# Loading a broadcast bias at another place of the POOL queue, in a linear-attention and gMLP block on Trainium2

## The chip, the cores and the metric

The kernel runs on one core of one Trainium2 chip. The core has a matrix engine (TensorE, PE in the profile), a vector engine (VectorE, DVE), an activation engine (ScalarE, ACT), a general engine (GpSimd, POOL) and SyncE (SP), which here only issues transfers. All five run their own instruction streams and wait for one another through semaphores. Transfers issued by SP, ACT or POOL share 16 DMA engines. The metric is the device time of one execution in microseconds (us), the median of several runs. The measurement of this kernel can tell a change of about 0.2%, some 0.5 us, from none.

## The reference

Two pre-normalised blocks, one after the other, on 2048 rows of 512 features (bf16). The first is linear attention with 32 heads of 16, the second a gated MLP whose gate mixes over the rows.

```python
x  = A_x
h  = x + A(layernorm(x))            # A: q,k,v = x @ wqkv; phi(t) = where(t>0, t+1, exp(t)) + 1e-6
                                    #    o = phi(q) @ (phi(k).T @ v) / (phi(q) . sum(phi(k)) + 1e-6); o @ wo
h2 = h + B(layernorm(h))
def B(x):
    z  = gelu(x @ w_in)             # 512 -> 1792
    z1 = z[..., :896]
    z2 = layernorm(z[..., 896:])
    g  = einsum('ts,sf->tf', w_sp, z2) + b_sp[:, None]   # mixes the 2048 rows; b_sp: one value per row
    return (z1 * g) @ w_out
```

The change concerns the load of `b_sp`, the mixing bias.

## The kernel before

The 2048 rows are 16 row tiles of 128, in four groups of four. The stages, which overlap:

- **x**: statistics of x on DVE, normalisation, transposition into `xT`.
- **k, q**: projections on PE, phi by ACT (Exp and Relu, L727 and L729) and DVE (L730, L733, L736). ACT and DVE pass the intermediate values through three buffers `e` (the pool `EB`).
- **kv and denominators**: L790 to L911.
- **h**: PE multiplies phi(q) by a matrix prepared from k, v and wo (L933, 8 matmuls for two row tiles). DVE adds x (L938) and makes the statistics (L577, L581). POOL makes 1/sqrt(var + eps) for two tiles at a time: an addition (L596), a power of -1/2 (L598, the "reciprocal root"), and with L631 and L632 the negative mean. ACT normalises into one of four buffers `xn` (L623), and SP transposes that by DMA into `hT` (L642).
- **z2**: PE projects each row tile of h (L968: 4 matmuls of 512 columns and 4 of 384), ACT applies gelu (L973), DVE makes statistics (L977, L581), POOL the roots (L596, L598 again), and DVE normalises in place (L612).
- **z1**: computed transposed, in 28 blocks of 4 matmuls (L999), gelu on ACT (L1004).
- **mixing**: PE multiplies z2 by the transposed `w_sp` (L1038, 28 sums over 16 row tiles each); DVE adds the bias (L1045, which reads `bsp`) and multiplies by z1. The first sum goes two row tiles at a time, in order, as z2 comes in. `w_sp` is transposed by 64 DMA transposes on SP (L1014, 16 for each group of output rows; the first mixing waits for all 16 of its group).
- **output**: L1056 projects with `wout`, L1062 adds h, SP stores.

The bias is broadcast to all 128 partitions, 512 KB in all. Its buffer lies in the store of the `e` buffers, as do the buffers `gb` and `o_` of the mixing and the output:

```python
bs_v = View(s_eb, 0, [S], BF16)
BS = Pool(1, lambda s, w: bs_v.ap, over=[EB])
```

`over=[EB]` means that the first operation on a tile of `BS` waits for every operation on every `e` tile. The load is a DMA issued on POOL, so POOL waits for this before it goes on with its queue.

The order of the work is written out. Each call of `op` adds an operation to a list, numbered as the program makes it; `ORDER` is a list of these numbers, and `schedule` gives each engine its operations in that order. `SLOT` holds, for each tile in the order of its first use, the buffer that it gets: a PSUM bank, an `e` or an `xn` buffer, and so on. `_waits` derives the semaphores from the data. The arguments `bias`, `cost` and `after` do not reorder anything here: `after` only demands that `ORDER` keep one operation behind another.

POOL also issues the loads of the weights (`wv`, `wo`, `win`, `wout`). The load of `wout` waits for the last transpose into `hT`, since `load` gets it as `behind`.

Of the kernel before, what the change touches and what calls it, by code (L numbers as in the profile page):

```python
# [10 lines left out]
P = 128  # L11
# [38 lines left out]
]  # L50
SLOT = [
# [6 lines left out]
]  # L58


# [294 lines left out]
def bass_sequential_preLN__linear_attn_block__mixer_gmlp__prompt_kernel(  # L355
# [11 lines left out]
    _, S, D = A_x.shape  # L367
# [61 lines left out]
    def small(shape, dtype):  # L429
        n = (int(np.prod(shape)) * mybir.dt.size(dtype) + GRAIN - 1) // GRAIN * GRAIN  # L430
        o = at[0]
        at[0] += n
        return View(s_sm, o, shape, dtype)
# [33 lines left out]
    BS = Pool(1, lambda s, w: bs_v.ap, over=[EB])  # L467
# [8 lines left out]
    def bank(i):  # L476
        return lambda a: a[:, i, :]
# [4 lines left out]
    g = Program(nc)  # L482
# [8 lines left out]
    def dve_c(n, mode=1):  # L491
        return 0.08 + 0.00103 * n / mode


    def load(eng, name, dst, src, nbytes, bias=0.0, behind=(), cost=0.5):
        o = op(eng, cost, lambda e: e.dma_start(dst.ap(), src), w=[dst], dma=(name, False), nbytes=nbytes,
               bias=bias, land=2.3)
        for p in behind:
            o.deps[p] = True
        return o  # L500
# [94 lines left out]
    def rstd_pool(var, dst, n):  # L595
        op("pool", 0.18, lambda e: e.tensor_scalar(dst.ap(), var.ap(), EPS_LN, None, op0=ALU.add), r=[var], w=[dst])  # L596
        h = nhalf[0:n]
        return op("pool", 0.665, lambda e: e.tensor_tensor(dst.ap(), dst.ap(), h.ap(), ALU.pow), r=[dst, h], w=[dst])  # L598
# [316 lines left out]
    for gs in DEN:  # L915
# [4 lines left out]
                    q_proj(gq, f)  # L920
        den(gs)

    for gq in range(NG):
        g.bias = -GROUP * gq
        for p in (2 * gq, 2 * gq + 1):
            t = Tile(PS, 2)
            for ti in range(2):
                n = 2 * p + ti
                l = pqT[gq][:, (n % TPG) * P:(n % TPG + 1) * P]

                def mm(e, t=t, ti=ti, l=l):
                    for c in range(KD):
                        i = e.matmul(t(bank(ti)).ap(), lhsT=l.ap()[:, c, :], rhs=mw[c, :].ap(), start=(c == 0),  # L933
                                     stop=(c == KD - 1))
                    return i
                op("pe", 4 * MM, mm, r=[l, mw.all()], w=[t()])
            d = x[2 * p:2 * p + 2, :]
            op("dve", dve_c(1024), lambda e, t=t, d=d: e.tensor_tensor(d.ap(), t().ap(), d.ap(), ALU.add),  # L938
               r=[t(), d], w=[d])
            rs = small([2], FP32)  # L940
            for n in (2 * p, 2 * p + 1):
                stats(x[n, :], Row(st_h, n))
                aggr(Row(st_h, n), 6)
            rstd_pool(st_h[2 * p:2 * p + 2, 7], rs.all(), 2)
            nm = small([2], FP32)
            if 2 * p in N2_ACT:
                minus(st_h[2 * p:2 * p + 2, 6], rs.all(), nm.all())
            for i in range(2):
                n = 2 * p + i
                t = Tile(XN)  # L950
                if n in N2_ACT:
                    normalise_act(t(), x[n, :], rs[i:i + 1], nm[i:i + 1])
                else:
                    normalise(t(), x[n, :], Row(st_h, n), 6, rs[i:i + 1])
                transposed(n, t, hT, n in H_BY_PE)
# [61 lines left out]
            after = [o]  # L1017
        return after

    bsp = Tile(BS)  # L1020
    behind = [last_T[xT[0].store]]
    for tg in range(NG):
        g.late = tg > 0
        behind = load_wsp(tg, behind + ([last_T[hT[0].store]] if tg == 1 else []))
        if tg == 0:
            load("pool", "bsp", bsp(), B_b_sp.partition_broadcast(P), P * S * 2, bias=-120.0, cost=1.0)

    last_mix = [None]

# [86 lines left out]
```

## Time and profile before

| what | value |
|---|---|
| median of 3 runs | 242.46 us (242.20 to 242.58) |
| the profiled execution's own time | 242.06 us |
| its span, first to last instruction | 240.8 us |
| busy share of PE, DVE, ACT, POOL | 98%, 55%, 33%, 14% |
| issue of the bias load on POOL | 91.22 us |
| issue of the `wout` load on POOL | 108.00 us |
| first mixing matmul | 116.07 us |

Times of the profile count from the first instruction of the span. In a timeline each row gives start, length, engine, line, operation, tiles out<-in, shape and count, and in brackets how long the engine stood idle before it and what it waited for. A matmul's row ends later than the next may start (its pipeline drains), so starts are compared with starts. A row with "q" behind the engine's name is of its queue, which only issues. In a view by groups, the columns behind the bar are busy time, mean ns of one, and idle time before them with its releaser. The view of waits gives total, number and longest. In the row of windows: stretch, its length, then for PE, weight loads, DVE, ACT and POOL the busy time with the number of instructions, then the granted clock of PE, the share of the DMA engines and GB/s.

### The profile page before, as it was taken

The page shows a single profiled execution, that of the slowest core. Times are in us where ns is not written, and L with a number is a line of the kernel's source. Part 1 is how long each engine was busy: PE and PEld are TensorE (multiplying, and loading weights), DVE is VectorE, ACT ScalarE, POOL GpSimd, SP SyncE. Part 2 cuts the span into 40 slices and gives each one's busy share as a digit, 9 for nine tenths or more (in the row PEclk, how much of TensorE's full clock was granted, in tenths as well). Part 3 has the DMA queues.
Part 4 walks back from the last instruction along what each step waited for, and adds up shares of the span by engine and source line. Part 5 has one row for each costly group of instructions (what it writes and reads, how often), then busy time and mean ns, then how long its engine had stood idle before and what let it go on. Part 6 is the DMA issues. An engine that isn't in the chain of part 4 may idle for free.

```text
span 240.8 us, 3059 instructions
## 1 busy us (share of the span) xinstructions
PE 235.8 (98%) x1200; PEld 110.4 (46%) x1200; DVE 132.5 (55%) x269; ACT 78.9 (33%) x102; POOL 34.7 (14%) x84
## 2 busy tenths in 40 slices
PE   7999999999999997999999999999999999999996
PEld 2664444544444553444444444444444444444443
DVE  3998882489999586298323233252332523323444
ACT  3795746686268789356140000000000000000000
POOL 7113412000421704037100000000000000000000
DMA  6943349960224446449544444445100100000022
GB/s 206 317 68 65 68 87 255 301 123 3 44 45 86 69 82 137 106 98 213 120 97 108 93 106 93 107 96 127 40 0 0 65 25 0 0 3 0 0 86 88
DMA packets 56702, 21.83 MB, mean 91 GB/s; under 512 B 50704, under 2 KB 55824, under 8 KB 56688
## 3 DMA queue, kind: packets, MB, share of 16 engines
q1 hardware_dynamic: 54928, 16.62, 31.9%
q0 software_dynamic: 944, 4.33, 6.0%
q10 hardware_dynamic: 816, 0.70, 1.0%
q8 instruction: 9, 0.15, 0.3%
q14 instruction: 5, 0.04, 0.1%
HBM read 7.47 MB, written 2.10 MB: 40 GB/s over the span
## 4 chain that ended last, share of the span: by engine, by line
PE 94%; DMA 3%; ACT 1%; DVE 1%; issue 0%
PE ps L1038 40%; PE ps L1056 10%; PE ps L999 10%; PE ps L968 8%; PE ps L769 6%; PE ps L790 6%; PE ps L933 6%; PE ps L751 6%; DMA hT<-xn 2%; DMA xh<-in_A_x_dram 1%; ACT pk_xn_z L973 1%; DVE small L577 1%; PE ps L651 1%; PE ps L882 0%; PE ps L862 0%; PE ps L806 0%
## 5 line engine op out<-in xcount | busy, mean ns | idle before, releaser
L1038 PE MATMUL ps<-wsp,pk_xn_z 128*128 128x512 bf16 x336 | 73.2, 379 | 0.0
L1045 DVE TENSOR_TENSOR e<-ps,e 128x512 bf16<-128x512 f32 x28 | 19.3, 691 | 67.7 <-PE ps L1038 67.7
L1038 PEld LDWEIGHTS ps<-wsp,pk_xn_z 128*128 128x128 bf16 x336 | 32.9, 98 | 39.6
L968 PE MATMUL ps<-win,hT 128*128 128x512 bf16 (+1 forms) x128 | 25.7, 352 | 1.8 <-DMA hT<-xn 1.8
L999 PE MATMUL ps<-hT,win 128*128 128x512 bf16 x112 | 25.6, 379 | 0.0
L1056 PE MATMUL ps<-wout,xT_pq_z 128*128 128x512 bf16 (+2 forms) x119 | 24.7, 366 | 0.0
L1038 PE MATMUL ps<-wqkv_wsp,pk_xn_z 128*128 128x512 bf16 x112 | 24.3, 379 | 0.0
L977 DVE BATCH_NORM_STATS2 small<-pk_xn_z 128x6 f32<-128x512 bf16 (+1 forms) x32 | 18.1, 606 | 10.2 <-ACT pk_xn_z L973 10.2
L577 DVE BATCH_NORM_STATS2 small<-xh 128x6 f32<-128x512 bf16 x32 | 20.7, 677 | 3.4 <-DMA xh<-in_A_x_dram 3.3
L727 ACT ACTIVATE e<-ps 128x1024 bf16<-128x1024 f32 x16 | 16.4, 1026 | 10.8 <-PE ps L751 8.6
L968 PEld LDWEIGHTS ps<-win,hT 128*128 128x128 bf16 x128 | 12.4, 98 | 14.4 <-ACT pk_xn_z L973 2.2
L1004 ACT ACTIVATE xT_pq_z<-ps 128x1024 bf16<-128x1024 f32 (+1 forms) x16 | 14.1, 917 | 12.3 <-PE ps L999 12.3
L1056 PEld LDWEIGHTS ps<-wout,xT_pq_z 128*128 128x128 bf16 x119 | 11.5, 98 | 13.0
L1062 DVE TENSOR_TENSOR e<-ps,xh 128x512 bf16<-128x512 f32 (+2 forms) x17 | 11.2, 660 | 11.3 <-PE ps L1056 11.3
L1038 PEld LDWEIGHTS ps<-wqkv_wsp,pk_xn_z 128*128 128x128 bf16 x112 | 11.0, 98 | 13.2
L999 PEld LDWEIGHTS ps<-hT,win 128*128 128x128 bf16 x112 | 11.0, 98 | 12.6
L598 POOL TENSOR_TENSOR small<-small 128x2 f32<-128x2 f32 x22 | 16.2, 742 | 1.0
L790 PE MATMUL ps<-pk_xn_z 128*128 128x512 bf16 x64 | 16.2, 379 | 0.0
L973 ACT ACTIVATE pk_xn_z<-ps 128x896 bf16<-128x896 f32 x16 | 14.2, 915 | 5.8 <-PE ps L968 5.8
L596 POOL TENSOR_SCALAR small<-small 128x2 f32<-128x2 f32 x22 | 6.8, 309 | 64.5 <-DVE small L581 64.2
L769 PE MATMUL ps<-xT_pq_z,wqkv_wsp 128*128 128x512 bf16 (+1 forms) x80 | 15.9, 337 | 0.0
L751 PE MATMUL ps<-wqkv_wsp,xT_pq_z 128*128 128x512 bf16 x64 | 15.6, 379 | 0.0
(71 smaller groups left out, 180.2 us busy)
## 6 DMA issues: line engine op xcount, KB each, us to landing
out_dram<-e SPq DMA_DIRECT2D x15, 128.0 KB, 1.7
win<-in_B_w_in_dram POOLq DMA_DIRECT2D x1, 1792.0 KB, 11.7
xh<-in_A_x_dram SPq DMA_DIRECT2D x4, 256.0 KB, 6.2
wout<-in_B_w_out_dram POOLq DMA_DIRECT2D x1, 896.0 KB, 6.0
wsp<-in_B_w_sp_dram SPq DMA_TRANSPOSE x48, 2.8
wqkv_wsp<-in_A_wqkv_dram ACTq DMA_DIRECT2D x1, 512.0 KB, 4.4
wqkv_wsp<-in_A_wqkv_dram SPq DMA_DIRECT2D x1, 512.0 KB, 5.6
xh<-in_A_x_dram SPq DMA_DIRECT2D x1, 512.0 KB, 7.4
```

The costliest lines, as they stand in the source:

```text
L577: op("dve", dve_c(512), lambda e: e.bn_stats(s6.ap(), src.ap()), r=[src], w=[s6])
L727: op("act", act_c(n), lambda e: e.activation(lo.ap(), t(flat).ap(), ACT.Exp), r=[t()], w=[lo])
L751: i = e.matmul(t(bank(ti)).ap(), lhsT=lhs.ap()[:, c - a, :], rhs=rhs.ap()[:, c - a, :], start=(c == 0), stop=(c == KD - 1))
L769: r_ = e.matmul(t(bank(i)).ap()[:, a:b], lhsT=lhs.ap()[:, c, :], rhs=rhs.ap()[:, c, :], start=(c == 0), stop=(c == KD - 1), skip_group_che ...
L790: r = e.matmul(txk[h](bank(i)).ap(), lhsT=xx.ap()[:, c * P:(c + 1) * P], rhs=kk.ap(), start=(n == 0), stop=(n == NT - 1))
L968: k = e.matmul(t(bank(i)).ap()[:, 0:b - a], lhsT=l.ap()[:, c, :], rhs=win[c, a:b].ap(), start=(c == 0), stop=(c == KD - 1))
L973: gelus.append(op("act", act_c(FH), lambda e, t=t, d=d: e.activation(d.ap(), t(flat).ap()[:, 0:FH], ACT.Gelu_apprx_tanh), r=[t()], w=[d], ...
L977: op("dve", dve_c(b - a), lambda e, s6=s6, src=src: e.bn_stats(s6.ap(), src.ap()), r=[src], w=[s6])
L999: k = e.matmul(t(bank(i)).ap(), lhsT=l.ap()[:, c, :], rhs=r_.ap()[:, c, :], start=(c == 0), stop=(c == KD - 1))
L1038: k = e.matmul(t(bank(0)).ap(), lhsT=l.ap()[:, s - a, :], rhs=r_.ap()[:, s - a, :], start=(s == 0), stop=(s == NT - 1))
L1045: op("dve", dve_c(512), lambda e: e.tensor_tensor(gb().ap(), t(bank(0)).ap(), bsp().ap()[:, tg * GW:(tg + 1) * GW], ALU.add), r=[t(), bsp( ...
L1056: k = e.matmul(t(bank(0)).ap()[:, 0:b - a], lhsT=l.ap()[:, fc, :], rhs=wout[fc, a:b].ap(), start=(fc == 0), stop=(fc == KF - 1))
```

## The change

The load of the bias is made at an earlier place of the program, and the first addition of each root pair of h is told to stay behind it:

```diff
         den(gs)
 
+    bsp = Tile(BS)
+    bsp_load = load("pool", "bsp", bsp(), B_b_sp.partition_broadcast(P), P * S * 2, cost=1.0)
+
     for gq in range(NG):
...
             rstd_pool(st_h[2 * p:2 * p + 2, 7], rs.all(), 2)
+            g.ops[-2].after.append(bsp_load)
             nm = small([2], FP32)
...
-    bsp = Tile(BS)
     behind = [last_T[xT[0].store]]
     for tg in range(NG):
         g.late = tg > 0
         behind = load_wsp(tg, behind + ([last_T[hT[0].store]] if tg == 1 else []))
-        if tg == 0:
-            load("pool", "bsp", bsp(), B_b_sp.partition_broadcast(P), P * S * 2, bias=-120.0, cost=1.0)
```

`ORDER` and `SLOT` are new lists as well, from about the twentieth microsecond of the work up to the first mixing sum. Number 293 is the load in the new one, and the former 293 to 602 are 294 to 603. The place of the load:

```diff
...
+    233, 264, 235, 256, 271, 234, 236, 272, 280, 309, 255, 273, 258, 294, 281, 274, 282, 295, 275, 310, 276, 296, 293,
+    283, 324, 284, 285, 414, 311, 325, 286, 339, 287, 299, 297, 288, 300, 298, 289, 340, 301, 312, 303, 354, 302, 292,
...
```

Read engine by engine, the new lists differ from the old ones so:

| engine | before | changed |
|---|---|---|
| POOL | bias load after the 32 instructions for h and the first two additions for z2; `wout` load after 8 of the 16 instructions for z2 | bias load ahead of the first addition for h; `wout` load ahead of all 16 instructions for z2 |
| SP | 10 transposes of `w_sp`, h tiles 0 to 7, two of `w_sp`, h 8 to 13, one, h 14 and 15, the rest | 8 of `w_sp`, h 0 to 12, three of `w_sp`, h 13 to 15, the rest |
| PE | L933 and earlier blocks; then z2 and z1 blocks mixed, two z1 blocks inside the first mixing | the same blocks, some neighbours swapped up to L933; from z2 tile 3 on another mixture; three z1 blocks inside the first mixing |
| ACT, DVE | follow PE's order | follow PE's new order; on ACT h tile 13 is normalised before 12 |
| buffers | mixing alternates PSUM banks 2 and 3 | 6 and 7; several `e` and PSUM tiles before that are dealt anew |

The mixing and the output keep their order on every engine.

68 rows, old and new, of tables (ORDER, SLOT) are left out of this document.

## The prediction

> **What bounds the kernel now.** The page first: how busy is each engine, and how long is the span?
>
> ```profile
> span 240.8 us, 3059 instructions
> PE 235.8 (98%) x1200; PEld 110.4 (46%) x1200; DVE 132.5 (55%) x269; ACT 78.9 (33%) x102; POOL 34.7 (14%) x84
> ```
>
> PE works 235.8 of 240.8 us, so an edit that leaves the matmuls alone can win only PE's idle time. The view of waits, for PE alone, says where that is:
>
> ```profile
> PE ps L968 <- DMA hT<-xn: 1.8, 1, 1.8
> PE ps L565 <- PEq L1101: 0.8, 1, 0.8
> PE ps L565 <- ACT small L593: 0.2, 1, 0.2
> PE ps L651 <- DVE pk_xn_z L612: 0.2, 1, 0.2
> ```
>
> After the start there is one wait: a z2 projection (L968) waits 1.8 us for a transpose into `hT`. PE's timeline gives its place and the unit costs that I use below.
>
> ```profile
> 65.76 3.19 PE L968 MATMUL ps<-win,hT 128*128 128x512 bf16 x16
> 68.79 1.89 PE L933 MATMUL ps<-pk_xn_z,xT_pq_z 128*128 128x512 bf16 x8
> 70.52 1.68 PE L968 MATMUL ps<-win,hT 128*128 128x512 bf16 x8
> 72.03 1.89 PE L999 MATMUL ps<-hT,win 128*128 128x512 bf16 x8
> 73.75 1.68 PE L968 MATMUL ps<-win,hT 128*128 128x512 bf16 x8
> 93.42 1.03 PE L999 MATMUL ps<-hT,win 128*128 128x512 bf16 x4
> 96.21 2.54 PE L968 MATMUL ps<-win,hT 128*128 128x512 bf16 x12 [1.76 <-DMA hT<-xn]
> 116.07 1.89 PE L1038 MATMUL ps<-wsp,pk_xn_z 128*128 128x512 bf16 x8
> ```
>
> From start to start, a tile's z2 projection (8 matmuls) takes 72.03 - 70.52 = 1.51 us, a z1 block (4 matmuls) half of 73.75 - 72.03, 0.86, and the 8 matmuls of L933 1.73. After the z1 block at 93.42 the next matmul was due at 94.28 and starts at 96.21: **1.93 us** lost, which is 1.76 plus the overlap of neighbouring rows. The granted clock was 1.00 in all windows that I asked for, this one too, so nothing else hangs on the gap:
>
> ```profile
> 90.00:95.00 5.00, 4.45 (x24) 2.06 (x22) 3.68 (x9) 5.00 (x8) 2.60 (x6) 1.00 0.65 146
> ```
>
> Why was it late? The chain that ended last, around that place, then POOL's timeline and the DMA issues (KB, us to landing):
>
> ```profile
> 89.08 1.73 ACT pk_xn_z L973 x2
> 90.80 0.70 ACT xn L623
> 91.50 0.03 ACT pk_xn_z L973
> 91.53 4.55 DMA hT<-xn
> 96.08 0.14 issue
> ```
> ```profile
> 59.78 0.76 POOL L596 TENSOR_SCALAR small<-small 128x2 f32<-128x2 f32 x1 [22.25 <-DVE small L581]
> 91.22 0.65 POOL L496 DMA_DIRECT2D e<-in_B_b_sp_dram  x1
> 108.00 1.01 POOL L496 DMA_DIRECT2D wout<-in_B_w_out_dram  x1
> ```
> ```profile
> e<-in_B_b_sp_dram POOLq DMA_DIRECT2D x1, 512.0 KB, 4.2
> hT<-xn SPq DMA_TRANSPOSE x16, 2.5
> ```
>
> Tile 13's transpose is issued at 91.53 and takes 4.55 us where the median of 16 is 2.5. The load of the bias is in flight from 91.22 + 0.65 = 91.87 to 91.22 + 4.2 = 95.4, and the transpose lands 0.7 us after it. With 2.5 it would have landed at 94.0, and with the 0.14 of issue PE could have started at 94.17, before 94.28.
>
> **The change, part by part.** *The load moves* ahead of 34 POOL instructions (the 32 that make roots for h, and two additions for z2), and now has only to wait until the `e` buffers are free. Their last reader and what follows on DVE:
>
> ```profile
> 55.32 0.69 DVE L733 TENSOR_TENSOR xT_pq_z<-e 128x1024 bf16<-128x1024 bf16 x1
> 55.93 2.35 DVE L938 TENSOR_TENSOR xh<-ps,xh 128x1024 bf16<-128x1024 f32 x2
> 59.39 0.30 DVE L581 BATCH_NORM_AGGREGATE small<-small 128x2 f32<-128x6 f32 x2
> ```
>
> That reader keeps its place on DVE and ends at 56.01. So the load is issued from 56.0 to 56.7 and lands at about 60.2. Behind it waits POOL's first addition for h, which needs the aggregate that ends at 59.69: 3.0 us of cover, cost nothing. The DMA is over before SP's first transpose of h:
>
> ```profile
> 62.79 14.87 SPq L642 DMA_TRANSPOSE hT<-xn  x8
> 77.70 2.57 SPq L1014 DMA_TRANSPOSE wsp<-in_B_w_sp_dram  x2
> ```
>
> The issue was not seen beside L938. Its bounds are 0.65 and the 1.01 of the `wout` load; both are covered.
>
> [...]
>
> *All orders are rewritten* (the list of numbers is a new one), and so a gain in one place can be lost in another. I decoded it by engine. Up to L933 PE's set of blocks is the same, with neighbours swapped; two things are closer than they were (ACT's copy for L819 now stands behind one more activation of q, and one `e` buffer serves several activations in a row); I put them at 0 to 0.1 us, from the 0.14 of issue above. At L968 the order differs from the fourth tile on, and I redo its due times by counting blocks from 65.76.
>
> *Tile 13*: ahead of it stand 13 projections, 10 z1 blocks and 8 matmuls of L933: 65.76 + 13 x 1.51 + 10 x 0.86 + 1.73 = 95.7. Its transpose: tile 5's projection ends at 65.76 + 5 x 1.51 + 7 x 0.86 + 1.73 = 81.1, 81.2 with its drain. Then ACT does, in order, two gelus for z2, one for z1, and four normalisations, 10, 11, 13, 12.
>
> ```profile
> 87.27 1.02 ACT L1004 ACTIVATE xT_pq_z<-ps 128x1024 bf16<-128x1024 f32 x1
> ```
>
> That is 2 x 0.87 + 1.02 + 4 x 0.70 = 5.6, so 86.8. SP issues tile 12, three transposes of `w_sp` that formerly stood elsewhere, then 13, 14, 15, at 2.57 / 2 = 1.29 each: tile 13 at 86.8 + 4 x 1.29 = 92.0, landed by 94.5. **1.2 us in hand.** Tile 15 is issued at 94.6, lands at 97.1 and is due at 95.7 + 1.51 + 0.86 = 98.1: 1.0 in hand. Nothing from POOL is in flight then, since `wout` waits for tile 15.
>
> *The wout load* moves on POOL ahead of all roots for z2, and waits there for tile 15's transpose: POOL is held until 97.1 + 1.0 = 98.1. Behind it queue the roots on which the first mixing needs its rows. The stage of before, 98 to 116, by groups (DVE and POOL), and what DVE waited for:
>
> ```profile
> L598 POOL TENSOR_TENSOR small<-small 128x2 f32<-128x2 f32 x6 | 4.6, 772 | 0.2
> L596 POOL TENSOR_SCALAR small<-small 128x2 f32<-128x2 f32 x5 | 1.8, 358 | 14.0 <-DVE small L581 13.8
> L612 DVE TENSOR_SCALAR pk_xn_z<-pk_xn_z,small 128x896 bf16<-128x896 bf16 x14 | 6.7, 501 | 1.5 <-POOL small L598 1.4
> L977 DVE BATCH_NORM_STATS2 small<-pk_xn_z 128x6 f32<-128x512 bf16 x5 | 3.2, 675 | 4.4 <-ACT pk_xn_z L973 4.4
> L977 DVE BATCH_NORM_STATS2 small<-pk_xn_z 128x6 f32<-128x384 bf16 x6 | 3.2, 543 | 0.0
> L581 DVE BATCH_NORM_AGGREGATE small<-small 128x2 f32<-128x12 f32 x8 | 1.4, 196 | 0.0
> ```
>
> The first mixing matmul comes at 116.07 - 1.93 - 0.86 = 113.3 (one z1 block more stands behind it than before), and tile 4's rows are needed two pairs of matmuls later, at 114.1. DVE, from tile 8's statistics to tile 4's normalisation, has 47 instructions: 9 x 0.675 + 13 x 0.543 + 14 x 0.196 + 11 x 0.501 = 21.4 us, or 17.6 if each overlaps its neighbour by 0.08, as 55.32 + 0.69 does the row at 55.93. They start when ACT is through with tile 8: tile 10's projection ends on PE at 65.76 + 10 x 1.51 + 7 x 0.86 + 1.73 = 88.6 (88.8 with drain), and four gelus of 0.87 follow: 92.3. So tile 4 is ready between 109.9 and 113.7, plus DVE's waits for POOL, 1.4 before. I take 112, near the lower end, since most of the 47 run back to back: 2 us in hand; at the other end, 115.1, it is 1.0 late. POOL's own part, 6 additions and 5 roots, is 6.0 us from 98.1 and mostly hides in that.
>
> *PSUM banks* are dealt anew (mixing alternates 6 and 7 instead of 2 and 3). It stays two banks in turn, at no cost. The last five `w_sp` transposes of the first group now stand behind tile 15:
>
> ```profile
> wout<-in_B_w_out_dram POOLq DMA_DIRECT2D x1, 896.0 KB, 6.0
> wsp<-in_B_w_sp_dram SPq DMA_TRANSPOSE x48, 2.8
> ```
>
> The last is issued at 94.6 + 5 x 1.29 = 101.1 and lands by 103.9, 0.7 us after `wout` (97.1 + 6.0 = 103.1) if that holds it up as the bias did tile 13. It is due at 113.3: nothing.
>
> **Sum.** The profiled run took 242.06 us (span 240.8): 242.06 - 1.93 = 240.13, with up to 0.1 for the new close call. It lies 0.40 under the median 242.46, so the median goes to 242.46 - 1.93 + 0.07 = **240.6 us**.
>
> **The rivals.**
> *Part of it stays or is given back.* The 1.0 us by which tile 4 is late at the slow end leaves 0.93 of the gain: 241.5. Or the load was only part of the cause. If the load and the transpose share the DMA engines half and half, the transpose's data time (2.5 less 1.29 of issue: 1.2) at most doubles; of the 2.05 us by which tile 13 was late, 0.85 then have another cause and may stay, the gain is 1.1, and the time 241.4. Against it: the landing follows the load's by 0.7 us, as if it had waited it out. [...]
>
> *No change:* the transposes are late again, for the three of `w_sp` that now stand before tile 13. It would take 1.2 us more for a first delay and 3.1 for all of the gain: 242.4. Against it: these have no POOL load beside them now.
>
> *Slower:* the `wout` load as POOL's head starves the first mixing. It decides from 3.9 us beyond my 112 (2.0 in hand and 1.93 won). If L598 and L596 cost double beside the busy DVE, 6.0 us more on POOL and nothing of it hidden, tile 4 is ready at 118, PE stands 3.9 us, and the time is 242.46 - 1.93 + 3.9 = 244.4. For it: all 16 POOL instructions of z2 now stand behind one wait, and the addition at 59.78 shows that one can take 0.76 where their mean is 0.36. Against it: in the rows of the stage the same instructions ran beside the same DVE work.
>
> **How the numbers follow.** Forecast 0.78 (240.2 to 240.9: 1.93 +- 0.2 and the spread of the three runs), part given back 0.10 (to 241.9), no change 0.05, slower 0.07. The measurement can tell about 0.2%, 0.5 us; so faster 0.88, same 0.05, slower 0.07. The range 240.2 to 241.5 leaves the last two out, and the slow edge of the second.
>
> **What would show it.** The bias load near 56.0 on POOL, landing near 60.2, with the first addition still at 59.8; tile 13's transpose at 2.5 us, no PE wait at L968; first L1038 near 113.3 and no wait of L1038 for DVE; span 238.9. It is wrong if PE waits for DVE L612 at L1038, if a transpose of h still lands late, or if the first root for h slips behind the load.

## The result, and the profile after

| kernel | median, us | range, us | runs | profiled run, us (span) | ratio to before [95%] |
|---|---|---|---|---|---|
| before | 242.48 | 242.2 to 242.7 | 6 | 242.06 (240.8) | 1 |
| after | 240.36 | 240.03 to 241.11 | 6 | 240.49 (239.2) | 0.9915 [0.9899, 0.9931] |

The kernel became 2.1 us faster, as forecast (240.6, with 240.2 to 241.5 as the range). The first lines of the page of after, and its waits of PE (us in total, times, longest):

```profile
span 239.2 us, 3060 instructions
PE 235.7 (99%) x1200; PEld 110.6 (46%) x1200; DVE 132.7 (55%) x269; ACT 79.1 (33%) x102; POOL 34.8 (15%) x84
```
```profile
PE ps L565 <- PEq L1102: 0.8, 1, 0.8
PE ps L651 <- DVE pk_xn_z L612: 0.4, 1, 0.4
PE ps L565 <- ACT small L593: 0.2, 1, 0.2
```

PE's work is the same to 0.1 us and the span is 1.6 us shorter, so all that changed is time in which PE stood. The wait of 1.8 us for `hT` has gone and none has come in its place. The windows of after around the old place (busy us of PE, PEld, DVE, ACT and POOL, granted clock, DMA share, GB/s) show PE without a gap, at a granted clock of 1.00:

```profile
90.00:95.00 5.00, 5.00 (x28) 2.55 (x26) 3.78 (x9) 4.93 (x8) 0.00 (x0) 1.00 0.47 102
```

In the edited kernel the line numbers are a little higher: the z2 projection is L972 (was L968), the z1 block L1003 (L999), the mixing L1039 (L1038), the `w_sp` transposes L1018 (L1014). The timelines of POOL, SP and PE, in order of time within each engine:

```profile
56.64 0.55 POOL L496 DMA_DIRECT2D e<-in_B_b_sp_dram  x1 [18.70 <-DVE xT_pq_z L733]
60.11 0.77 POOL L596 TENSOR_SCALAR small<-small 128x2 f32<-128x2 f32 x1 [2.92 <-DVE small L581]
...
97.64 1.04 POOL L496 DMA_DIRECT2D wout<-in_B_w_out_dram  x1 [14.94 <-DMA hT<-xn]
63.02 25.26 SPq L642 DMA_TRANSPOSE hT<-xn  x13
88.33 3.87 SPq L1018 DMA_TRANSPOSE wsp<-in_B_w_sp_dram  x3
92.24 3.89 SPq L642 DMA_TRANSPOSE hT<-xn  x3
66.10 3.19 PE L972 MATMUL ps<-win,hT 128*128 128x512 bf16 x16
94.40 1.89 PE L1003 MATMUL ps<-hT,win 128*128 128x512 bf16 x8
96.13 4.05 PE L972 MATMUL ps<-win,hT 128*128 128x512 bf16 x20
113.62 1.46 PE L1039 MATMUL ps<-wsp,pk_xn_z 128*128 128x512 bf16 x6
```

The bias load is issued as soon as DVE's L733 frees its buffers, and POOL then still stands 2.92 us for DVE's aggregate: the load cost POOL nothing. Tile 13's transpose is issued at 92.24 and, by the list of DMA issues (KB left out for transposes, us from issue to landing), takes its 2.5 us again; its projection starts at 96.13, and not for want of it.

```profile
hT<-xn SPq DMA_TRANSPOSE x1, 2.5
```

### The profile page after: what moved, and what is told of

Same layout as the page of the kernel before. It is cut to its first block, busy times and chain, and to the rows that moved or that the text cites. A ratio compares the mean times of both kernels' runs of the same rounds, so it can differ in the third digit from the quotient of the medians.

```text
span 239.2 us, 3060 instructions
## 1 busy us (share of the span) xinstructions
PE 235.7 (99%) x1200; PEld 110.6 (46%) x1200; DVE 132.7 (55%) x269; ACT 79.1 (33%) x102; POOL 34.8 (15%) x84
## 4 chain that ended last, share of the span: by engine, by line
PE 97%; DMA 1%; DVE 1%; issue 0%
PE ps L1039 40%; PE ps L972 10%; PE ps L1057 10%; PE ps L1003 10%; PE ps L751 6%; PE ps L769 6%; PE ps L790 6%; PE ps L936 6%; DMA xh<-in_A_x_dram 1%; DVE small L577 1%; PE ps L882 0%; PE ps L651 0%; PE ps L862 0%; PE ps L806 0%; PE ps L843 0%; DVE pk_xn_z L612 0%
## 5 line engine op out<-in xcount | busy, mean ns | idle before, releaser
L1039 PE MATMUL ps<-wsp,pk_xn_z 128*128 128x512 bf16 x336 | 73.2, 379 | 0.0
L1039 PEld LDWEIGHTS ps<-wsp,pk_xn_z 128*128 128x128 bf16 x336 | 32.9, 98 | 39.6
L972 PE MATMUL ps<-win,hT 128*128 128x384 bf16 (+1 forms) x128 | 25.5, 352 | 0.0
L1003 PE MATMUL ps<-hT,win 128*128 128x512 bf16 x112 | 25.5, 379 | 0.0
L1039 PE MATMUL ps<-wqkv_wsp,pk_xn_z 128*128 128x512 bf16 x112 | 24.3, 379 | 0.0
L972 PEld LDWEIGHTS ps<-win,hT 128*128 128x128 bf16 x128 | 12.5, 98 | 12.2
L598 POOL TENSOR_TENSOR small<-small 128x2 f32<-128x2 f32 x22 | 17.0, 776 | 1.0
L1039 PEld LDWEIGHTS ps<-wqkv_wsp,pk_xn_z 128*128 128x128 bf16 x112 | 11.0, 98 | 13.2
L1003 PEld LDWEIGHTS ps<-hT,win 128*128 128x128 bf16 x112 | 10.9, 98 | 12.8
L751 PE MATMUL ps<-wqkv_wsp,xT_pq_z 128*128 128x512 bf16 x64 | 15.6, 379 | 0.1
L936 PE MATMUL ps<-pk_xn_z,xT_pq_z 128*128 128x512 bf16 x64 | 14.5, 379 | 0.0
```

The costliest lines, as they stand in the source:

```text
L751: i = e.matmul(t(bank(ti)).ap(), lhsT=lhs.ap()[:, c - a, :], rhs=rhs.ap()[:, c - a, :], start=(c == 0), stop=(c == KD - 1))
L972: k = e.matmul(t(bank(i)).ap()[:, 0:b - a], lhsT=l.ap()[:, c, :], rhs=win[c, a:b].ap(), start=(c == 0), stop=(c == KD - 1))
L1003: k = e.matmul(t(bank(i)).ap(), lhsT=l.ap()[:, c, :], rhs=r_.ap()[:, c, :], start=(c == 0), stop=(c == KD - 1))
L1039: k = e.matmul(t(bank(0)).ap(), lhsT=l.ap()[:, s - a, :], rhs=r_.ap()[:, s - a, :], start=(s == 0), stop=(s == NT - 1))
```

## Experiments

**Theory:** the bias load, in flight beside tile 13's transpose, is the whole cause of the gap; taking it away from there is the whole gain, and where it goes matters little. **Rivals:** the gain comes from the rewritten order (1.2 us in hand for tile 13) rather than from the load; or the load and the transpose only share the DMA engines, so that part of tile 13's lateness is of another kind. In the diffs, 603 is the load's number in the list of before.

**1. The load alone moved, the order of before kept** (`e1_load_alone`)

```diff
-    ... 339, 299, 297, 300, 302, 301, ... 426, 458, 408, 603, 485, 500, ...
+    ... 339, 299, 297, 603, 300, 302, 301, ... 426, 458, 408, 485, 500, ...
```


> The order of before, with the load of the bias alone moved ahead of POOL's first addition for h; PSUM banks and all other places as before. Theory (the load held up tile 13's transpose): the transpose takes 2.5 us again and lands at 94.0, PE's wait at the z2 projection goes, 1.9 us faster, about 240.5. Rival A (the rewritten order made the gain, by asking for tile 13 later): the wait stays, 242.4. Rival B (load and transpose only shared the DMA engines, 0.85 us of the lateness had another cause): 1.1 us faster, 241.4.

Measured: 240.25 us (240.13 to 240.67, 5 runs), ratio 0.9906 [0.9892, 0.9921]: the time of after. PE's timeline:

```profile
93.93 1.03 PE L999 MATMUL ps<-hT,win 128*128 128x512 bf16 x4
94.80 2.54 PE L968 MATMUL ps<-win,hT 128*128 128x512 bf16 x12
```

The projection that stood 1.76 us now starts 0.87 after the z1 block, which is the block's own length. Everything else in the list of numbers is as before, so the whole gain is the load's place and the rest of the rewritten order is worth nothing that can be measured. What the new order does give is room: here tile 13's transpose lands at 94.45, 0.35 ahead of its reader; in after it lands at 94.74 for a reader at 96.13.

**2. The load late instead of early** (`e3_load_late`): before's order, with the load directly ahead of the `wout` load.

```diff
-    ... 426, 458, 408, 603, 485, 500, ... 473, 474, 523, 586, 445, 429, ...
+    ... 426, 458, 408, 485, 500, ... 473, 474, 523, 603, 586, 445, 429, ...
```


> The order of before, with the load of the bias moved the other way, directly ahead of the wout load on POOL (issued near 106, landed near 111, first used near 120). Theory: any place away from the transposes of h will do: 1.9 us faster, about 240.5, as in the run with the load moved early. Rival (the early place itself is what helps): no gain, or slower if DVE waits for the bias at the first mixing sum, 242.4 or more.

Measured: 240.61 us (240.48 to 241.01, 6 runs), ratio 0.9924 [0.9911, 0.9938]. POOL's timeline:

```profile
106.80 0.65 POOL L496 DMA_DIRECT2D e<-in_B_b_sp_dram  x1
107.45 0.97 POOL L496 DMA_DIRECT2D wout<-in_B_w_out_dram  x1
```

Fifty microseconds later does as well as early. So "as soon as the buffer is free" is not the point; "not beside a transpose that PE is about to need" is. For here the load did lie beside transposes, those of `w_sp`: the one issued at 107.44, between this load and the `wout` load, took 9.1 us, and PE waited for none of them.

**3. The load back in the new order** (`e2_load_back`, `e5_load_back2`). The first try missed its place: in the renumbered list, 586 is a gelu of ACT and not `wout`, so the load (293 there) went out at 110.13.

```diff
-            g.ops[-2].after.append(bsp_load)
+    bsp_load.deps[gelus[8]] = True
```


> The order of after, with the load of the bias put back among the transposes of h: it waits for the gelu of tile 8, so that it is issued near 92.3, when tile 13's transpose is issued, and lands near 96.5; the wout load stays behind it. Theory: tile 13's transpose lands 0.65 us after the load, near 97.1, where PE asks for it at 96.1: a wait of 1.0 to 1.3 us, about 241.5. Rival A (the order made the gain): no wait, 240.4. Rival B (sharing): the transpose's data time of 1.2 us at most doubles, it lands by 95.9, no wait, 240.4.

Measured: 240.37 us (240.22 to 240.66, 5 runs), ratio 0.9912 [0.9899, 0.9926]. It says no more than the second experiment: the late load cost nothing here. The second try hung the load behind the twelfth gelu and put it ahead of `wout`, which is 587 there.

```diff
-            g.ops[-2].after.append(bsp_load)
+    bsp_load.deps[gelus[11]] = True
```


> The order of after, with the load put back among the transposes of h, at the place that the run e2 missed: directly ahead of the wout load on POOL, waiting for the gelu of tile 11, so issued near 91.8 and landed near 96.0, as tile 13's transpose is issued near 92.2. Theory (a transpose that meets a POOL load ends only after it): tile 13 lands near 96.6 instead of 94.7, PE asks for it at 96.1 and waits about 0.6 us: 241.0. Rival A (the rewritten order is what removes the wait): tile 13 lands in time, no wait, 240.4. Rival B (half and half sharing): it lands by 95.9, no wait, 240.4.

Measured: 241.61 us (241.09 to 242.75, 12 runs) beside 242.45 of before (29 runs), ratio 0.9968 [0.995, 0.9986]; the profiled run took 241.32. The timelines of POOL and PE, and the list of DMA issues in that stretch:

```profile
92.00 0.64 POOL L496 DMA_DIRECT2D e<-in_B_b_sp_dram  x1 [9.32 <-ACT pk_xn_z L976]
94.37 1.89 PE L1003 MATMUL ps<-hT,win 128*128 128x512 bf16 x8
97.02 2.32 PE L971 MATMUL ps<-win,hT 128*128 128x512 bf16 x11 [0.75 <-DMA hT<-xn]
```
```profile
e<-in_B_b_sp_dram POOLq DMA_DIRECT2D x1, 512.0 KB, 4.2
hT<-xn SPq DMA_TRANSPOSE x1, 4.7
```

The wait comes back with the load. The reader was due at 94.37 + 8 x 0.216 = 96.10 and starts at 97.02: 0.9 us, where 0.6 had been expected; the profiled runs differ by 0.8 (241.32 - 240.49), the medians by more, 1.25 (241.61 - 240.36), with runs that scatter over 1.7. The new order's room absorbs the rest of the transpose's extra 2.2 us.

**4. Two loads, one behind the other** (`e4_two_loads`): before with a second load of the same 512 KB, which nothing reads.

```diff
             load("pool", "bsp", bsp(), B_b_sp.partition_broadcast(P), P * S * 2, bias=-120.0, cost=1.0)
+            bsp2 = Tile(B2)
+            load("pool", "bsp2", bsp2(), B_b_sp.partition_broadcast(P), P * S * 2, bias=-120.0, cost=1.0)
```


> Before, with a second load of the same 512 KB right behind the first one, into a part of the same store that is free then (nobody reads it). Theory (a transpose ends only after the POOL loads in flight): the second load lands some 2.5 us after the first, near 98, tile 13's transpose 0.65 us after that, and PE waits about 4.4 us instead of 1.9: about 245. Rival B (sharing): the transpose's data time can at most double whatever is queued behind, it lands near 96.1 as before, 242.5.

Measured: 245.19 us (244.29 to 246.34, 4 runs), ratio 1.0113 [1.0086, 1.014]. The list of DMA issues, PE's timeline, and three windows with the clock (the 1.00, 0.77 or 0.50 behind POOL's count):

```profile
hT<-xn SPq DMA_TRANSPOSE x1, 6.1
```
```profile
93.64 1.03 PE L1001 MATMUL ps<-hT,win 128*128 128x512 bf16 x4
97.95 3.98 PE L970 MATMUL ps<-win,hT 128*128 128x512 bf16 x12 [3.28 <-DMA hT<-xn]
```
```profile
96.00:97.00 1.00, 0.00 (x0) 0.00 (x0) 0.93 (x2) 0.04 (x1) 0.00 (x0) 1.00 1.03 363
97.00:97.90 0.90, 0.00 (x0) 0.00 (x0) 0.85 (x3) 0.00 (x0) 0.00 (x0) 0.77 1.26 253
...
99.00:100.00 1.00, 1.00 (x4) 0.36 (x3) 0.00 (x0) 0.00 (x0) 0.00 (x0) 0.50 0.57 129
```

The second load lands at 97.65 and the transpose at 97.81: its landing came only when both were through. The time is the one expected, but not by the way expected. The gap is 97.95 - 93.64 - 0.86 = 3.45 us, less than forecast, and near its end the granted clock falls to 0.50, where it stays for 3.4 us: the twelve matmuls take 3.98 us instead of 2.54, another 1.4. The mean of 0.77 over 97.00 to 97.90 puts the fall at about 97.5 (an estimate), some 3.0 us after PE's last matmul (94.50); the 1.93 of before left the clock at 1.00.

**5. Half the load** (`e6_half_load`): 256 KB early, 256 KB at the old place.

```diff
-            load("pool", "bsp", bsp(), B_b_sp.partition_broadcast(P), ...)
+            for i in range(2):
+                c = slice(i * S // 2, (i + 1) * S // 2)
+                load("pool", f"bsp{i}", bsp(lambda v, c=c: v[:, c]), B_b_sp[c].partition_broadcast(P), ...)
```


> The order of before, with the load cut into two halves of 256 KB: one moved early, ahead of the first addition for h, the other left at its old place. Theory: the half moves its data in about half of the 2.5 us, lands near 94.3, tile 13's transpose 0.2 to 0.7 us after it, between 94.5 and 95.0, so PE waits 0.3 to 0.8 us instead of 1.9: about 241.0. Rival B (sharing, and 0.85 us of another cause): 0.85 + 0.6 us late against 94.0, a wait of 1.3 us, 241.8.

Measured: 242.03 us (241.5 to 242.54, 12 runs), ratio 0.9979 [0.9966, 0.9992]: 0.4 us saved, and nearer to the 241.8 of the sharing rival than to the 241.0 of the theory. DMA issues and PE's timeline:

```profile
e<-in_B_b_sp_dram POOLq DMA_DIRECT2D x1, 256.0 KB, 3.4
```
```profile
94.62 1.03 PE L999 MATMUL ps<-hT,win 128*128 128x512 bf16 x4
96.61 2.54 PE L968 MATMUL ps<-win,hT 128*128 128x512 bf16 x12 [0.96 <-DMA hT<-xn]
```

The order of the landings held: the half lands at 95.83, the transpose 0.64 later, at 96.47. The size did not: half the bytes take 3.41 us where the whole takes 4.21, and the theory had counted on half of the data's 2.5 us. A straight line through these two sizes would leave 2 x 3.41 - 4.21 = 2.6 us that do not go with the size (an estimate). PE's gap is 96.61 - 94.62 - 0.86 = 1.13 instead of 1.93, near the rival's 1.3; what speaks against the rival here is the landing just behind the load's, and that experiment 1 leaves nothing of the delay. The smaller gap would be worth 0.8 us; the profiled run lost 0.9 at its start, in a wait that before has not, so its total does not show this; whether the other runs had that wait is not known.

**6. Smaller pieces** (`e9_packets_512`, `e10_packets_256`): the same half, as every other stretch of 256 or of 128 columns.

```diff
-                c = slice(i * S // 2, (i + 1) * S // 2)
+                v2 = lambda v, i=i: v.rearrange("p (a b k) -> p a b k", b=2, k=256)[:, :, i, :]     (or k=128)
```


> As the half load (half the bias early, the other half at its old place just ahead of tile 13's transpose), but the halves are every other stretch of 256 columns, so the late half goes in 512 packets of 512 bytes instead of 128 of 2 KB; a transpose of h moves some 512 packets of 256 bytes. If the engines take turns packet by packet, 32 packets of the load and 32 of the transpose on each engine now alternate, and the transpose ends about when the load does: landing between 0.5 us ahead of the load's and 0.3 us behind it, where it was 0.64 us behind with 2 KB packets. If the transpose simply waits until the load is over, it lands about 0.65 us after the load again, whenever that is. Time in either case between 241 and 243 us, as the load itself may take longer in small packets; the order of the two landings decides.

> The same with every other stretch of 128 columns: the late half goes in 1024 packets of 256 bytes, twice as many as the transpose has. Turns packet by packet: the transpose is done when the load is about half through, and lands ahead of the load, by 0.5 us or more. Waiting until the load is over: it lands about 0.65 us after it, and PE waits as long as the load takes, 2 us or more.

Measured: 242.52 and 242.45 us (one run each, beside 243.16 of before). PE's waits and the DMA queues of the stretch (packets, MB, share of 16 engines) for 512 bytes, then for 256:

```profile
PE ps L968 <- DMA hT<-xn: 1.7, 1, 1.7
```
```profile
q1 hardware_dynamic: 1085, 0.26, 47.1%
q0 software_dynamic: 80, 0.26, 26.2%
```
```profile
PE ps L968 <- DMA hT<-xn: 1.5, 1, 1.5
```
```profile
q1 hardware_dynamic: 1088, 0.26, 41.2%
q0 software_dynamic: 80, 0.26, 19.9%
```

The loads landed at 96.00 and 95.91, the transposes at 96.56 and 96.45: 0.56 and 0.54 us behind, as with the plain half, and not ahead. But the edit did not do to the queue what it was to do: the load's queue shows 80 packets in both, as it does for the plain half (64 of 4 KB and 16 small ones), while the transposes' queue shows over a thousand. The pieces were never made, so these runs do not test what smaller pieces would do; the last section reads from the packets of before who went first.

**7. The cover used up** (`e7_hold_pool`): after, with 12 memsets on POOL behind the load; they fill parts of `hT` that the transposes overwrite later.

```diff
+    for i in range(12):
+        d = hT[1 + i // KD][i % KD, :]
+        op("pool", 0.46, lambda e, d=d: e.memset(d.ap(), 0.0), w=[d])
```


> After, with 12 idle memsets on POOL behind the load and ahead of the first addition for h, into parts of hT that are not yet in use: POOL is held from 57.2 to about 62.7, as if the load's issue had taken 6 us. It measures the cover at the new place. Theory (3.0 us of cover on POOL and 0.5 us in front of the first z2 projection): the first addition is 2.6 us late, PE waits 2.1 us at its first z2 projection: 242.4. Rival (the roots for h have more room than that): no wait, 240.4.

Measured: 242.95 us (242.55 to 244.24, 10 runs), ratio 1.0028 [1.001, 1.0047]. Timelines of POOL, SP and PE:

```profile
57.51 5.67 POOL L929 MEMSET hT<- 128x512 bf16 x12
63.14 0.24 POOL L597 TENSOR_SCALAR small<-small 128x2 f32<-128x2 f32 x1
66.03 14.44 SPq L643 DMA_TRANSPOSE hT<-xn  x7
68.56 3.19 PE L977 MATMUL ps<-win,hT 128*128 128x512 bf16 x16 [1.98 <-DVE xT_pq_z L912]
```

This run's load is 0.33 us later than that of after (56.97 against 56.64). Against after, shifted by that, the first addition for h is 2.7 us late (63.14 - 60.44), and the first z2 projection 2.13 (68.56 - 66.43). So of 5.67 us of work, 3.0 were free on POOL and another 0.6 between the first transpose's landing and its reader. The row names a DVE instruction as the releaser, but tile 0's transpose, issued at 66.03, landed at 68.47, later than that instruction's end (68.38). The whole run lost a little more than these 2.13: the profiled one took 2.42 more than after's (242.91 - 240.49), and the 0.33 of the later load makes up the difference.

**8. The load from ACT's queue** (`e8_act_queue`): before's order, the load issued by ACT, in its program directly behind tile 13's normalisation.

```diff
-            load("pool", "bsp", bsp(), ...)
+            load("act", "bsp", bsp(), ...)
-    ... 426, 458, 408, 603, 485, 500, 395, 396, 486, ...
+    ... 426, 458, 408, 485, 500, 395, 396, 603, 486, ...
```


> The order of before, with the load of the bias issued by ACT instead of POOL at the same time: directly behind the normalisation of tile 13, near 91.5, when SP issues that tile's transpose. Theory as the runs so far have it (a transpose ends only after the load in flight), if it holds for any load: tile 13's transpose lands 0.2 to 0.7 us after the load and takes 4 us or more, PE waits about as before, and ACT is 0.5 us later behind its issue: 242.5 to 243. If it holds only for loads that POOL issues: the transpose takes 2.5 us, no wait for it: about 240.5 to 241.

Measured: 240.5 us (240.19 to 240.73, 4 runs), ratio 0.9912 [0.9895, 0.993], and PE does not wait. From the time alone one would say that a load from ACT's queue leaves transposes in peace. The trace says otherwise. The timelines of ACT and SP, and the list of DMA issues in flight from 90 to 91:

```profile
89.71 0.39 ACTq L496 DMA_DIRECT2D e<-in_B_b_sp_dram  x1
90.52 0.91 ACT L973 ACTIVATE pk_xn_z<-ps 128x896 bf16<-128x896 f32 x1
91.31 0.81 ACT L623 ACTIVATE xn<-xh,small 128x512 bf16<-128x512 bf16 x1
89.17 1.27 SPq L642 DMA_TRANSPOSE hT<-xn  x1
```
```profile
e<-in_B_b_sp_dram ACTq DMA_DIRECT2D x1, 512.0 KB, 3.8
hT<-xn SPq DMA_TRANSPOSE x1, 4.5
```

(PE's L968 of tiles 13 and 12 starts at 94.91.) The load was issued at 89.71, ahead of the normalisation (91.31) that stands before it in ACT's program, and so it met tile 12's transpose instead of tile 13's. That one was issued 0.54 us before the load and yet took 4.5 us: it landed at 93.67, 0.17 behind the load's 93.50. Tile 12's projection stands behind tile 13's, at 94.91 + 1.51 = 96.42, so 2.7 us were in hand. Here the load from ACT's queue went with a transpose of 4.5 us, as POOL's did in before (4.55); this one could afford it.

## Why the prediction was right

**The cause.** "With 2.5 it would have landed at 94.0": experiments 1 and 2 take the load away by two routes and the transpose takes 2.4 us both times, with no wait. The term of 1.93 us is the whole change: 242.06 - 1.93 + 0.07 = 240.20 for the profiled run, which took 240.49; the 0.29 is a later start, below. The ratio's interval gives 1.7 to 2.4 us.

**The load's new place.** Forecast issue 56.0, landing 60.2, cover 3.0 us; measured 56.64, 61.04 and 2.92. The landing is 0.84 later: by the 0.34 of the next point, by 0.3 more at the issue, and by 0.2 for a flight of 4.40 us instead of 4.21. The issue took 0.55 us beside DVE's L938 (L941 in after, 56.26 to 58.61), below the 0.65 to 1.01 that bounded it; it ended at 57.19, while L941 ran on: no hold shows.

**The due times.** Everything in after lies about 0.34 us later than forecast from the start of L968's stage (66.10 where 65.76 was counted from): PE's wait at L651 is 0.4 instead of 0.2. That is not the new order: the last run of experiment 6, in before's order, has the same 0.4. With that taken off, tile 13 is issued at 91.9 (forecast 92.0), its reader starts at 95.8 (95.7), the first mixing matmul at 113.28 (113.3), and `wout` is issued at 97.3, so POOL is held until 98.3 (98.1). Of the 0.34, 0.27 are there at the first L751 matmul already (6.62 against 6.35, the earliest start of all the profiles). The 0.07 that came after it looks like the 0 to 0.1 set for the new close calls, but does not show them: from that matmul to the first L968 before took 59.41 us and after 59.48, and runs in before's order took 59.46 (experiment 1) to 59.88 (experiment 2). So that term came out by chance; no run shows that the close calls cost anything.

**The rivals.** Tile 4's rows, the point on which the slower case hung, were normalised by 112.2, due at 114.5; forecast 112 and 114.1, both before the shift. DVE's last stretch ahead of the mixing shows why the low end was the right one, eight normalisations back to back:

```profile
110.90 3.42 DVE L612 TENSOR_SCALAR pk_xn_z<-pk_xn_z,small 128x896 bf16<-128x896 bf16 x8
```

The sharing rival (half and half, so that 0.85 us would have had another cause) is out: without the load nothing of the delay is left. Half and half was the author's assumption, and no run shows it. The profile counts 144 packets of the load (128 of 4 KB) against over 500 of a transpose, and for most of the load it shows no sharing at all: from 92.5 to 94.2 before moved 107 of the load's packets and none of a transpose (last section). Whether the transpose's packets stood ready by then, no run shows.

**What was off, without effect.** The first group's last `w_sp` transpose behind tile 15 was to land by 103.9. Issued at 101.38, it landed at 106.76: the ones issued beside the 896 KB of `wout` landed one after another from 104.49, behind its own landing at 104.46. It was due at 113.6, so nothing showed. And the room that the new order gives tile 13, 1.2 us in the forecast, was no part of the gain: experiment 1 has the gain without it.

## What to carry to other kernels

When one transfer in a series takes much longer than its median, look for another queue's load in flight across it, and compare the two landings: if the slow one always ends a fraction of a microsecond behind the other (0.16 to 0.66 us in the table below), move the load to a stretch where nobody waits for a transfer; here its exact place there made no difference that could be measured (240.25 us early, 240.61 late). Halving such a load helped little (0.4 of 2.1 us), as its duration fell only from 4.2 to 3.4 us. A time that does not move can also mean that the delay fell on a transfer with slack (experiment 8: 240.5 us, with a transpose of 4.5 us that had 2.7 in hand), so read which transfer was hit before calling a queue harmless.

## What the runs showed of the hardware that was not expected

| load beside a transpose | load lands | transpose lands | behind by | issue to landing of the transpose |
|---|---|---|---|---|
| before, 512 KB from POOL | 95.43 | 96.08 | 0.65 | 4.55 |
| experiment 3, 512 KB from POOL | 96.22 | 96.88 | 0.66 | 4.67 |
| experiment 5, 256 KB from POOL | 95.83 | 96.47 | 0.64 | 3.74 |
| experiment 6, 256 KB in pieces | 96.00, 95.91 | 96.56, 96.45 | 0.56, 0.54 | 4.44, 4.30 |
| experiment 4, second of two | 97.65 | 97.81 | 0.16 | 6.06 |
| experiment 8, 512 KB from ACT | 93.50 | 93.67 | 0.17 | 4.49 |
| none in flight (tile 13 in after, experiments 1 and 2) | | | | 2.4 to 2.5 |

- In every row of the table the transpose lands behind the load, whichever engine issued the load. Where the load had 0.2 to 0.3 us of head start, the transpose ends 0.5 to 0.7 behind; where the transpose was issued 0.34 or 0.54 ahead of the load that ends last, 0.16 to 0.17. With more of a head start it need not be so: in experiment 1 a `w_sp` transpose issued 0.67 ahead of the `wout` load landed 2.9 us ahead of it (109.64 and 112.56).
- What came late differs. In before, with the load issued first, it was the transpose's data. From 92.5 to 94.2 only one queue moved anything, the load's (packets, MB, share of 16 engines):

```profile
q0 software_dynamic: 107, 0.44, 93.1%
```

  The first packet of the transpose comes at 94.27, 2.7 us after its issue; in experiment 1, without the load, 1.2 us after. In experiment 8, with the transpose issued first, its data moved first. The transposes' queue there from 90.2 to 92.4, and from 92.4 to 93.2, where the load ends:

```profile
q1 hardware_dynamic: 512, 0.13, 30.6%
q1 hardware_dynamic: 32, 0.00, 2.2%
```

  The 128 KB were through by 92.4, and only the 32 last packets, small ones, came after that, by the load's end. Why they moved in this order is not shown.
- A transpose was slow without a load, too. In after one transpose of h, issued at 79.38 with no load of the program in flight, took 4.1 us; a 16 KB transfer of the instruction queue fell into it. No run tests whether that is the cause.
- Half a load takes 3.41 us where the whole takes 4.21; in stretches of 512 or 256 bytes the half takes 4.19 and 4.07, though its queue shows 80 packets each time.
- In experiment 8 ACT issued the load 1.6 us ahead of an activation that stands before it in its program (89.71 and 91.31); the load's place in ACT's list was not its time.
- Behind a PE gap of 3.45 us the granted clock was 0.50, and the twelve matmuls took another 1.4 us (experiment 4: 3.98 us for 2.54); behind one of 1.93 us it was 1.00, and they took 2.54 (before).
